# The tail unit of the first batch becomes a group of its own at the beginning of the second exponential phase

## The chip, the cores and the metric

The kernel runs on one core of a Trainium2 chip. The metric is the device time of one execution in microseconds (us), lower being better. Five engines work side by side, each through its own instructions in a fixed order: TensorE (PE) for matrix products and transposes, VectorE (DVE), ScalarE (ACT), GpSimd (POOL) and SyncE (SP). POOL and SP issue the transfers. An engine waits at an instruction until the semaphores that it needs are up, and everything behind that instruction on the same engine waits with it.

## The reference

Attention with a window and a distance bias is followed by an expert layer without routing, on the attention's output.

```
batch, heads, seq, head_dim = 8, 8, 576, 64
scores = q @ k.T / 8 - slope[h] * |i - j|, kept where 0 <= i - j < 128
attn   = softmax(scores) ;  x = (attn @ v), heads joined: 4608 tokens x 512
h = x @ w_in            # 512 -> 2048
g = h * cos(h)
out = g @ w_out         # 2048 -> 512
```

Inputs and result are float32; the kernel works in 16-bit types with 32-bit sums.

## The kernel before

**Units of attention.** Each batch has 576 queries. Its work is cut into nine units: for each of four pairs of heads (`pr`) two units of 256 queries (`G` 0 and 1), and one unit `"t"`, the tail, which has the last 64 queries (512 to 575) of all eight heads. For a unit the steps are: scores on PE (L539, the tail's L529), an exponential on ACT out of the sums in PSUM (L598, the tail's L590), a multiplication by the mask with the distance bias on DVE (L623, the tail's L611), the product with v on PE (L653 and L656, the tail's L640 and L642), a division by the row sums on DVE (L694 and L696, the tail's L681 and L684), and the transposition of x into `xT`, in which x is the input of the expert layer. That last step has two forms: four or two PE transposes and a copy (`x_pe`: L742, or L729 for the tail, and the copy L752 on ACT or L753 on DVE), or a transposing transfer on SP (`x_dma`: L768, L762 for the tail). Which of them a unit takes is decided in `attention` by whether its tokens belong to a chunk (`first`) more than one chunk ahead of the phase.

**Chunks and phases.** The expert layer works through the 4608 tokens in nine chunks of 512. ACT must load a table to go from the exponential to the cosine and back, so the exponentials are gathered in phases. The program has a first phase (number -1 in the code) before any expert work, and then for each chunk c: the first half of the expert layer with its cosines (`moe1_half` L975 for chunk 0, `moe1` L782, `moe1_fast` L876), the attention phase c with `QUOTA[c]` units, and the second half (L1161 for chunk 0, L1067 later). So the "second exponential phase" is phase 0, between the cosines of chunk 0 and those of chunk 1. q and k of batches 0 and 1 are transposed by PE (`qk_transposes` L483, and copies L500 on ACT or L501 on DVE), those of later batches by SP (L396, L399) from `qnat` and `knat`, which POOL fills (L385).

**What sets the order.** The code writes the operations one after the other, but none is issued in that order. `TABLE` is a packed list of numbers: it gives the order in which `Plan.follow` takes the operations, and for those that may run on ACT or DVE it says on which. Semaphores for all dependences are then put in. So a change of one constant comes with a whole new table, and the order of all five engines is new; where a copy runs (L500/L501, L752/L753, L1052/L1053) is a choice of the table as well.

**Groups.** `attention` takes the units in twos. In a phase from 0 on, both units' scores are one operation, and the product with v of both is one operation too, unless one is a tail. In phase -1 each unit's scores are their own operation. The first phase has nine units before the change: the eight of the pairs and the tail of batch 0. The tails use two PSUM banks for the product with v.

Of the kernel before, what the change touches and what calls it, by code (L numbers as in the profile page):

```python
# [14 lines left out]
B, H, S, D = 8, 8, 576, 64  # L15
# [12 lines left out]


TABLE = (  # L30
    'c-nPV2Y6If7JmPfH!Wo*A%PHdEHqifjs=k}tV#(GFqBXPBn4$bu`FK_%_4*%1ObV(K#D*JSt&-E!h-'
    '0xDvPKfD@{Z`QYO7kX6D^JciMYzU|;fHUhcd1+;jf_Kj&N_3_w#jJy552L+3%Pc;zlP#H-yktj(-'
    'pEjqM{ck}PJwCrB3q-'
    '{9M;&d$5qHR9WADS}~;_2H1xbO#`q+wdtgon`B>6%HyG|f?3%VnDsdnr<5N0St5ZZ)?8zmXNGD<Zg2=y6N`U+Gy?'
    '$F$*GyJWJoN!r+3anTS_iMU&FrmJy)q1{k##U*rYHRJHq^Dy35b!Y@oPU}o$A?_9;n<O%5Xs0l2&{m^^1BgNm_9P'
    '~pqObs4C1TN&{Qy{6(86~%nA#%H5NW^O=4`d2vLnc~h(_}2&mQcz_^`@$G{b79x#rnLjt-93Hcj0-'
    'yv%|m2e+*e0cZK}!+72b)WUaJT8@pXD+fk0N6bOV1gB(Si4?NA5T2-'
    '!JB(zEKr!Mj%{>;HUNYjab!Z7$qCql;L3G!CjefR+FFk(bw73vr<2ntCbb8MB)_5dQYyf6J%<J=0tY;ul(MgN&rc'
    'O0s&EiG$uIcm#Y~Vab;v#yqnaVrE7GY>V-A}Btqa`;P_Nv&jvF#{*7WM`>VMkre&#)Wy?uO_aV#gax-'
    'm{4=v5trFP6j>R?Tw2c0rY#J*M(j<PaOY>o)>#w^hUa2)xJ2kX>J~-'  # L40
    '#3SczLYEI#)13`0UMgZCvSU&r@KXVhQx8AYHOt^~S#t385v1pL)39f1&X4(!RY_VSn%~;N7Le~0Vt5k)3C!7qncH'
    'Sb_KKyP6<WQBL=(H{om`}^2hwehkBNkN1f6-'
    '=6Jf`#n1*9F&|{#~8ip5b`?XFO3>mnmKg4fqM&X#D2BXTu`vb#MxEL-'
    '2=FZh<=U!>)?uhVjo~ev?pC0h90j^d!W2#$W>Vg}3Lez;yMB~`dF58D5!*GHZ4bkokcrZJo8XMBIs3+J`c0!*&!='
    'cNak2M(+9t6%k<c;_TI5&xT-;_~SjMe)zLQ?kr-'
    '9G)}so_oZgT~!nS)>B%(>F{i(nL<%Kma6dPT_kIY8xqVGm@6sSZY)QY;}3kyZHF!JjrNbPWohF6A1kpQae^Jz>4Y'
    'nMq|4ag_#Z%abX$X0Qx{bdg5-'
    'w!C^Sy0wzSSv6YO*7!5g5KOZPW>L)jeqDWi^PVfHiNt_&bV&I7<#pb?el1f*R3lvbBscPqQM6(|M=#E!7MQtWiEo'
    '^$q8jetWg{{laSk`ID;w6<lHL!It@CI3ZRWxET-dy=6bdfZi^BN)-'
    'kx6rkxYh^Af7Y$CX%W0qP@nf!;+_cuy#JAV$$(>L5)aS8M@n1a32RRL3Yb{W0a`!VJ8|o4{JEnxs(L});p(&v8a9'  # L50
    'u_yO{KZHL$YuW?tu(Sy-'
    '!vCGTmAdZpg4wXLtycpkG<<E5@OtDZg=!_1h1+Njmjw*z0aL)7QnhFOPv(elHPlI>oe%EXgvk}suL+RHI+l!oPEe'
# [43 lines left out]
class Plan:  # L96
# [63 lines left out]
    def follow(self, text):  # L160


        raw = zlib.decompress(base64.b85decode(text))
        n, at, self.order = len(raw) // 2, 0, []
        assert n == len(self.all)
        for lo, hi in zip(raw[:n], raw[n:]):
            at = (at + lo + 256 * hi) % 65536
            o = self.all[at % 32768]
            if isinstance(o.fn, dict):
                e = "dve" if at >= 32768 else "act"  # L170
                o.fn, o.eng = o.fn[e], (e,)
            self.order.append(o)

# [79 lines left out]
def bass_alibi_sliding__then__act_gcu_kernel(  # L253
# [8 lines left out]
    with ExitStack() as ctx:  # L262
        def sb(name, shape, dt=BF16):
            return ctx.enter_context(nc.sbuf_tensor(name, shape, dt))

        R = Plan(nc, ctx)
# [20 lines left out]
        xT = sb("xT", [128, NPAIR, XR], F16)  # L287
# [7 lines left out]
        qB = {w_: gsum[:, 2304 * i:2304 * i + 2304].bitcast(BF16).rearrange("p (y c) -> p y c", y=2)  # L295
              for i, w_ in enumerate("qk")}
# [1028 lines left out]
```

## Time and profile before

| | before |
|---|---|
| median of three runs | 300.12 us (299.69 to 300.17) |
| profiled execution | 299.71 us |
| its span | 298.0 us |
| PE busy | 287.9 us, 97% |
| DVE busy | 262.1 us, 88% |
| ACT busy | 222.1 us, 75% |
| POOL busy | 95.2 us, 32% |
| moved by the DMA engines | 37.96 MB |
| TensorE clock granted | 1.00 |

The span is the time from the first to the last instruction of the profiled execution; 1.7 us lie around it in that execution's time. A busy row is the sum over the instructions of an engine. In a row of the timeline stand the start, the length, the engine, the line, the operation, and behind `x` how many like instructions follow one another; in brackets stands how long the engine had waited before, and whose result ended that wait. Matrix products overlap in PE's pipeline: the length of a row holds the last one's passage, so the pitch of a stream is read from starts.

### The profile page before, as it was taken

The numbers are of one execution on the slowest core, as the hardware profiler recorded it, in microseconds if no ns is written. First come the engines' busy times: TensorE is split into PE (matmuls) and PEld (weight loads), VectorE is DVE, ScalarE is ACT, GpSimd is POOL, SyncE is SP. The second block draws the span as 40 slices with busy tenths as digits, with TensorE's granted clock in tenths as the row PEclk, the third lists the DMA queues.
The fourth block names the chain that finished last, engine by engine and source line by source line (L and its number), as shares of the span: only waits on it lengthen the run. The fifth ranks groups of instructions, "written<-read, shape, count | busy, mean of one in ns | idle before, by whom it ended". The sixth has DMA issues, their size and how long they took to land.

```text
span 298.0 us, 7278 instructions
## 1 busy us (share of the span) xinstructions
PE 287.9 (97%) x2974; PEld 205.2 (69%) x2974; DVE 262.1 (88%) x522; ACT 222.1 (75%) x318; POOL 95.2 (32%) x122
## 2 busy tenths in 40 slices
PE   2899999999999999999999999999999999999996
PEld 2678845446874586458854788547768888888884
DVE  3879877599977999899999999999999999999972
ACT  5788878689757889688777878579778758778620
POOL 7997000599642303991195005000000000000000
PEclk9999999999999999999999999999999999999999
DMA  7999999999999994999999939973131400041033
GB/s 153 173 205 208 207 169 146 180 196 155 136 175 147 130 187 90 142 173 173 169 170 133 163 85 130 159 164 74 21 79 21 150 2 0 2 141 37 10 134 106
DMA packets 147729, 37.96 MB, mean 127 GB/s; under 512 B 133360, under 2 KB 146416, under 8 KB 147696
## 3 DMA queue, kind: packets, MB, share of 16 engines
q0 software_dynamic: 99344, 18.10, 79.7%
q1 hardware_dynamic: 48352, 19.41, 34.5%
q8 instruction: 23, 0.38, 0.5%
q14 instruction: 10, 0.08, 0.1%
HBM read 36.70 MB, written 9.44 MB: 155 GB/s over the span
## 4 chain that ended last, share of the span: by engine, by line
PE 94%; DVE 2%; POOL 1%; issue 1%; ACT 1%; POOLq 0%; DVEq 0%
PE ps L1067 33%; PE ps L782 24%; PE ps L876 11%; PE ps L539 5%; PE ps L975 5%; PE ps L1161 4%; PE ps L653 3%; PE ps L656 2%; PE ps L742 2%; PE ps L483 2%; PE ps L529 1%; DVE kt L501 1%; PE ps L640 1%; PE ps L642 1%; PE ps L1138 1%
## 5 line engine op out<-in xcount | busy, mean ns | idle before, releaser
L1067 PE MATMUL ps<-w_outb,gT 128*128 128x256 f16 x512 | 82.3, 273 | 0.0
L782 PE MATMUL ps<-xT,w_inb 128*128 128x512 f16 x336 | 82.2, 379 | 0.0
L787 ACT ACTIVATE cos<-ps,halfpi 128x512 f32<-128x512 f32 x84 | 54.9, 687 | 18.9 <-PE ps L782 13.9
L598 ACT ACTIVATE p<-ps 128x768 bf16<-128x768 f32 (+1 forms) x64 | 55.6, 915 | 11.5 <-PE ps L539 9.5
L791 DVE TENSOR_TENSOR gT<-ps,cos 128x512 f16<-128x512 f32 x84 | 54.5, 686 | 5.5 <-ACT cos L787 5.1
L1067 PEld LDWEIGHTS ps<-w_outb,gT 128*128 128x128 f16 x512 | 48.2, 98 | 12.5 <-issue 1.3
L782 PEld LDWEIGHTS ps<-xT,w_inb 128*128 128x128 f16 x336 | 31.7, 98 | 31.1 <-DVE gT L791 1.5
L375 POOL DMA_DIRECT2D vp<-in_v_dram x40 | 34.3, 892 | 53.1 <-PE ps L656 35.3
L1067 PE MATMUL ps<-wsum,gsum 128*128 128x256 f16 x256 | 38.5, 273 | 0.0
L623 DVE TENSOR_TENSOR p<-p,emask 128x768 bf16<-128x768 bf16 (+1 forms) x64 | 38.0, 615 | 0.3
L385 POOL DMA_DIRECT2D qnat<-in_q_dram x30 | 25.5, 918 | 23.9 <-DMA qt<-qnat 23.9
L1052 ACT ACTIVATE ob<-ps 128x512 f32<-128x512 f32 x33 | 19.6, 598 | 13.7 <-PE ps L1067 11.2
L385 POOL DMA_DIRECT2D knat<-in_k_dram x30 | 25.7, 948 | 9.3 <-DMA kt<-knat 7.0
L1067 PEld LDWEIGHTS ps<-wsum,gsum 128*128 128x128 f16 x256 | 23.2, 98 | 4.0 <-issue 0.5
L876 PE MATMUL ps<-xT,w_inb 128*128 128x256 f16 x132 | 24.8, 273 | 0.0
L696 DVE TENSOR_TENSOR xnats<-ps,rec 128x256 f16<-128x256 f32 x56 | 21.9, 420 | 0.5
L539 PE MATMUL ps<-qt,kt 64*128 64x128 bf16 (+1 forms) x320 | 20.1, 253 | 1.3 <-DVE kt L501 1.3
L653 PEld LDWEIGHTS ps<-vp,p 128*128 128x128 bf16 x256 | 16.0, 99 | 4.3 <-issue 1.0
L653 PE MATMUL ps<-vp,p 128*128 128x65 bf16 x256 | 18.9, 196 | 0.1
L1067 PE MATMUL ps<-wsum,gT 128*128 128x256 f16 x112 | 18.1, 273 | 0.0
L539 PEld LDWEIGHTS ps<-qt,kt 64*128 64x128 bf16 x320 | 11.9, 98 | 8.6 <-issue 3.6
L1161 PE MATMUL ps<-w_outb,gT 128*128 128x512 f16 x64 | 17.6, 380 | 0.0
(111 smaller groups left out, 478.0 us busy)
## 6 DMA issues: line engine op xcount, KB each, us to landing
out_dram<-ob SPq DMA_DIRECT2D x35, 256.0 KB, 2.7
vp<-in_v_dram POOLq DMA_DIRECT2D x32, 128.0 KB, 6.9
qnat<-in_q_dram POOLq DMA_DIRECT2D x24, 128.0 KB, 7.1
knat<-in_k_dram POOLq DMA_DIRECT2D x24, 128.0 KB, 10.8
w_inb<-in_moe_w_in_dram POOLq DMA_DIRECT2D x4, 512.0 KB, 10.5
w_outb<-in_moe_w_out_dram POOLq DMA_DIRECT2D x4, 512.0 KB, 21.8
gsum<-in_q_dram POOLq DMA_DIRECT2D x1, 576.0 KB, 15.5
gsum<-in_k_dram POOLq DMA_DIRECT2D x1, 576.0 KB, 17.6
```

What stands on the lines that cost most here:

```text
L375: op("pool", [lambda e, t=t, rows=rows: e.dma_start(vp[b % 2][0:rows, t, :, 0:64], v[b, :, 128 * t:128 * t + rows, :].rearrange("h p d -> ...
L385: fns.append(lambda e, t=t, rows=rows: e.dma_start(nat[which][b % 2][0:rows, t, :, :], src[b, :, 128 * t:128 * t + rows, :].rearrange("h p ...
L539: ins = e.matmul(ps[:, banks[x], c0:c1], keys_ap(b, x, pr, kc), query_ap(b, x, pr, qb, 128 * nb), start=c0 == 0 and (b, pr, G) not in seed ...
L598: op("act", lambda e: e.activation(P[i][:, :, 0:hi], src_[:, :, 0:hi], ACTF.Exp, scale=0.125), w=held + [("P", i)], occ=920 if G else 691, ...
L623: op("dve", lambda e: e.tensor_tensor(p, p, m, ALU.mult), r=[("EM", h0), ("EM", h1)] + ([] if G else [("EM2", h1)]), w=[("P", i)], occ=600 ...
L653: ins = e.matmul(o, P[i][:, x, d0:d0 + 128], V[:, kc, h, 0:65], start=True, stop=not two)
L782: op("pe", lambda e, kc=kc: e.matmul(ps[:, bank, :], w_in[:, kc, 128 * fc:128 * fc + 128], xT[:, kc, r0:r0 + CH], start=(kc == 0), stop=(k ...
L787: op("act", lambda e: e.activation(cosb[ci][:, :], ps[:, bank, :], ACTF.Sin, bias=halfpi[:, 0:1]), r=["halfpi"], w=[("B", bank), ("cos", c ...
L791: op("dve", lambda e: e.tensor_tensor(gT[gi][:, fc, :], ps[:, bank, :], cosb[ci][:, :], ALU.mult), r=[("cos", ci)], w=[("B", bank), ("g", ...
L876: op("pe", lambda e, i=i, kc=kc: e.matmul(ps[:, bank, 256 * i:256 * i + 256], left(kc, p0 + i), right(kc), start=(start and i == 0 and kc ...
L1067: op("pe", lambda e, t=t, p=p: e.matmul(ps[:, bank, 256 * t:256 * t + 256], left(p, slice(128 * t, 128 * t + 128)), right(p), start=(start ...
L1161: op("pe", lambda e, t=t, fc=fc, bank=bank: e.matmul(ps[:, bank, :], gT[gi][:, fc, 128 * t:128 * t + 128], w_out[:, fc, :], start=(fc == 0 ...
```

## The change

The constant `QUOTA[0]` goes from 8 to 9 units and the first phase takes eight units instead of nine. A table `TRI` gives the sizes of the first groups of a phase: phase 0 begins with a group of one, which is the tail of batch 0, and goes on in twos. Since the tail's phase is now 0 and its tokens lie in chunk 1, `first > phase + 1` no longer holds for it, and its x goes by `x_pe` instead of `x_dma`. `TABLE` is new as a whole; the other edits make the group sizes a list.

```diff
 TABLE = (
...
-                e = "dve" if at >= 32768 else "act"
+                e = "dve" if at >= 32768 else o.eng[0]
...
-        QUOTA = [8, 10, 10, 12, 14, 9]
+        QUOTA = [9, 10, 10, 12, 14, 9]
...
+        TRI = {0: [1]}
...
         def attention(us, phase):
 
-            for g in range(0, len(us), 2):
-                two = us[g:g + 2]
+            sizes = TRI.get(phase, [])
+            sizes = sizes + [2] * ((len(us) - sum(sizes) + 1) // 2)
+            for i, size in enumerate(sizes):
+                g = sum(sizes[:i])
+                two = us[g:g + size]
...
-                    if g // 2 < SEEDN.get(phase, 0):
+                    if i < SEEDN.get(phase, 0):
...
-        attention(every[0:9], -1)
-        done = 9
+        attention(every[0:8], -1)
+        done = 8
```

In the changed file the lines stand 7 to 11 further down: L590 is L598 there, L598 is L606, L975 is L983.

PE at the end of the first phase, from the second pair's product with v (L656) to the first expert products; before:

```order
L656 MATMUL ps<-vp,p 128x65
L539 MATMUL ps<-qt,kt 128x256 x2
L539 MATMUL ps<-qt,kt 128x128 x4
L742 MATMUL ps<-ident,xnats 128x128 x8
L539 MATMUL ps<-qt,kt 128x256 x2
L539 MATMUL ps<-qt,kt 128x128 x4
L529 MATMUL ps<-qt,kt 128x64 x16
L975 MATMUL ps<-xT,w_inb 128x256 x7
```

and now:

```order
L664 MATMUL ps<-vp,p 128x65
L750 MATMUL ps<-ident,xnats 128x128 x4
L547 MATMUL ps<-qt,kt 128x256 x2
L547 MATMUL ps<-qt,kt 128x128 x4
L983 MATMUL ps<-xT,w_inb 128x256
L750 MATMUL ps<-ident,xnats 128x128 x4
L547 MATMUL ps<-qt,kt 128x256 x2
L547 MATMUL ps<-qt,kt 128x128 x4
L983 MATMUL ps<-xT,w_inb 128x256 x12
```

The tail's 16 products (L529) are gone from here, and one expert product moved ahead of the last transposes and scores.

ACT in the same place, from the second pair of exponentials to the table of the cosine; before:

```order
L500 ACTIVATE qt<-ps 128x4x32x5
L598 ACTIVATE p<-ps 128x2x384 x2
L598 ACTIVATE p<-ps 128x1024 x3
L752 ACTIVATE xT<-ps 128x256 x3
L590 ACTIVATE ptail<-ps 128x1024
L598 ACTIVATE p<-ps 128x1024
L752 ACTIVATE xT<-ps 128x256
L980 ACT_TABLE_LOAD
```

and now:

```order
L508 ACTIVATE qt<-ps 128x4x32x5
L606 ACTIVATE p<-ps 128x2x384
L508 ACTIVATE kt<-ps 128x4x32x5
L606 ACTIVATE p<-ps 128x2x384
L606 ACTIVATE p<-ps 128x1024 x2
L760 ACTIVATE xT<-ps 128x256
L606 ACTIVATE p<-ps 128x1024
L760 ACTIVATE xT<-ps 128x256
L606 ACTIVATE p<-ps 128x1024
L988 ACT_TABLE_LOAD
```

The tail's exponential (L590) left; a copy of transposed keys (L500, formerly one of DVE's L501) came to ACT, and two of the copies to `xT` went elsewhere.

PE where phase 0 begins, between the last products of chunk 0's first half (L975) and the first scores of batch 1; before:

```order
L483 MATMUL ps<-ident,gsum 64x128 x16
L975 MATMUL ps<-xT,w_inb 128x256 x7
L1161 MATMUL ps<-w_outb,gT 128x512 x2
L640 MATMUL ps<-vp,ptail 128x65
L642 MATMUL ps<-vp,ptail 128x65
```

and now:

```order
L491 MATMUL ps<-ident,gsum 64x128 x16
L983 MATMUL ps<-xT,w_inb 128x256 x11
L1169 MATMUL ps<-w_outb,gT 128x512 x5
L491 MATMUL ps<-ident,gsum 64x128 x16
L537 MATMUL ps<-qt,kt 128x64 x16
L1169 MATMUL ps<-w_outb,gT 128x512 x12
L547 MATMUL ps<-qt,kt 128x256 x2
L547 MATMUL ps<-qt,kt 128x128 x2
```

Before, the tail's product with v (L640, L642) stood here; now its scores (L529) do, and its product with v and the transposes of its x (L729, four of them) come behind the first scores of batch 1.

More of the change, by code (lines that the diff above doesn't have):

```diff
@@ L38 @@
[L38 to L52, printed above, removed]
@@ new lines @@
+    'PRx1#wipsW2&0QZI+rrmw_yEnwGF8!`QcsjSc-+E7o9{#=ezxpHoHajOBH-'
+    'G=TwwoSucrE{|`QGbqJa#6duFnI$n9oI<>qxDW7QK>gMUPS?X_33>oH3*t{bIC6_I%7tN!1wX8$Z3Adq;+zUI`f|'
+    'Mwd(L+&hlWlYfQBKOlqJeNZqcfLho!N;j^hU(Q!_E84)vkR!Sk2ss&290%D^F<<XbRxRnJq`l|;oymOVLY;quF1%'
+    'Xjcfk)h7h2;huHrkX<7%{lwZfI<+%S9^RmInFWm;YMqh@VTwf7au`^JZt1A4FP94Li$XyKhcp9Y_6I?Ct!X$?MT8'
+    't|<Le^JBx)1GvGyCH9FA+?^LgM`ms&AUGDx*u-'
+    'Nf#O`)(D8Upb<jYYn?fVgX~(=2>ZFo`>s!aRH?0_QYI$=ID!zO`)aUkMbf>6K3g|^;VH(#9KP8m5OiWWrgbK9(-'
+    'vuQU?W0tQXVh}8O1Yv;rq{|eam53o^5k}$Y0h@*slc_5eh^>^0%{XdF!kOa5LbNld<x!(OU3ICdZfr(J(4%f`}5}'
@@ new lines @@
+    'P^uje=N*qa%ZQ4qZ+$-'
+    '9pmf!aRHqH@z*D3595wm~(LUioezHduTx*~1<qOO9EW}(v+>6_egBV7+{#D=_$#W8u1#Fq4AZ{0Fbg4mM8B1D&^i'
+    '=XbUyYK7~gv0H7GxnGNk`1KiI3ao8CeKu?DO_8Ct^1P>&zf~}E_DKkx&6+anN`83fJleGEGb<rzA@`m#I;2?J}eo'
+    'bn0;w!<KjlA2k}jhF8Dor9iqrQC{;2IUq4Q(ney)`goxbxiZM_bhJ<cvT~k2+kfYQ=ry28HY2bEE@43%c@Sty+K6'
+    '%;2F0X%#QYm;V&guEP;?dwEKN+El`F-'
+    '+meMC3({0QEg>!ck8gk#A^L0@+<{X0|#k=D2e&cfn2&rE+&N$k6K$%_IfYSHKlZE$_?u~jF<ey8Jmqy?eU<Ev_;f'
+    'PCSQtZOZ=N}C}6B(5k?wm;)g1d28TdAbA~+q`|x0n#5XuGVVS$q%hN5LF>qB}Z-=a5VXVA-'
@@ new lines @@
+    '(;g+8|hUF&z)5R=ju0Y4fzj4h@ShoZIbrJ@|#7&KqZgo2N8&9skPxXmrs(bI<#qcl1^i{{<(G+{L``&}pfsRH-'
+    '4;r8j06xN=_OvOQ75ytkSsW6|erLDwI6bzp#Bce0_zPfD`>!7ZIuRvZYWu1DE&A*Ds&emD;8<J?-'
+    '6DuEQERA?Q$B}))gGzgiX9XxRl5BrcI-'
+    '68<~Me1G%gcL&rq^Ju)|7+6<Y19&q;h*osI4x0D_7!(N>!=AdOwgii8L1GL*0H3&M6~d<+d@)vuAP<PKt)8oFD|V'
+    'n97G;BTz+;ywMk#wmWn&KQVy<{6m(=lb7-A(SNw?GJ9cKFv{yT#cj^q6?5+EhF?-'
+    '{IV_Ui^D0kJQ$EhbnI?u%&8sFx$7y(PJE*xJv=o1p*za%!aRopP|`h2Pu0Wk*dFG;gJs)K4*QX#(DmEyClJF}E3N'
+    'c%qeoIB%N*{FwlFYkjRg07L!f4qq`hZ5Q)1ERV>wOnl&g(I<Qw+^B!t^$|Xjmqar91c4l&2vZWp76_U%0ZP9*@^B'
@@ new lines @@
+    '$-HyVo2R8200@5~-'
+    'TMLf%Ww`a^<VRxjk$w`r06HNKt;4px_{Gzayco#XpRr#+1E+N|!Kap|9Qo>ma3xoPu8N2<VQ_h*Oj8mIIOiwjZ9w'
+    'rrN=fYVF+fM9e?uVJuB7HgRD}Vj5;b)yesZC6*uivK{0KIERMw*r2j;x%l%(9~l;8Qk-zSzwig)+ACW-'
+    'O+zmo}^SsMVg{P46tp6GNCq?W`Ac4g|2mqFH;w`TWV;J%kOH?1Hozte%*k)I^ky@TumK<2(rHvQpNwzw*_Xwd(%_'
+    'qFa22kp5P+ouKAe3zTGb0glpn|r};`xLR?8NsH_-'
+    'Po{xtWw1_aK-&)(T~PI`*G=GpHsonSyQwv!WW~zUeNJ<RI}{Hhv*(Ppp|(|KO(#Qfk-VFoO8cN#z#=Dmt)(Y+Fjn'
+    'P6e@8jiT9gKM*x)YcxsJE(!1dA#XwMXV$mvn?J8k8X_9!t>!Rd&1!HJ1pBN#<#bqFh2&g6i=NAH3J{ALguU@-'
@@ new lines @@
+    '27(jQCoSqQ`l8tOOP(C;iaau%piM$9Xx^Z@8{P7ZjC_sXqN`as~u2Q<3-'
+    'n}%kW7#{QQ3j)6?TOI*Bw+KOKao5Iwu`rX6RNALJJ^5_K_uP}Nt~@Ox*I(^EV?ZIy}zL}N3MQYn(Nl>q#*(<(?mC'
+    '3eQWg7S2M>GpI`qt*Z1cKz|fD~^LTfrzCT1HAlD~z7q(`5{z`SZdVcEV0*~iIl!M0;OnPdVR2<cU3BzSe-'
+    'tKsc3BO(TuG-c*R`J6`+4`(um%SYa*CX`A_I#pcaU)Z(?ffgO-Gyz1SW63yq|$H4_Igsmd$*B{)<pNFSMQ8Wf1Pk'
+    '_-'
+    '5%%8#C3;=P1a;xWcmCr5P|Z@{@Sn!zfIT`{`2GtM2ZVujokXh?ZoN?6nRVgDly|*Wb7vq1T^XlT!gq3B_0kz&xFI'
+    'FxQ$<Y>0SHp3vv=rxu)-wehrQT^BdO|jKoXtd&?bb0=MmW+%(ZAAH%#gIPJU?N5?NiH5SvuPD|!CjC-'
@@ new lines @@
+    'YTUyF`*e#{_&_P6}+nH?UshC?=*A?%8<bNTWUhKm1Rh8=36e8IBl)W1GT}_DGK>HhN-Zvou~@!Vy!e-'
+    '_`U_lo>J&X^^5M=NkGV#}f{RLy<3K{H1^BHplXql}T~3GA++WEApYTvP=(DW)@}bGmqhzjX0!_7}6e1ZaL;AMcJm'
+    'ZPDm~ThaO@X&vIsaV=^_n;LsyXH)CFkX-'
+    '!#Yq92W+m|QS==(o&?D3c9ke$QN~aWe8XM`1Ik7y+5wP|Ts`r5h~PW(T&R7Hn;fIGLH2rBFt6C`+Jb>@A6+Y%o%c'
+    'kQq?e+ExfD131iOnrCKVXk9-'
+    'eG>Vx`mTQ|KBfS>?6gXzCFumAknZpc=V}+K(2#%QzD_d+`jC3<VFyY1ulC^j?NhmA8HU`;N!34&R@f0g;vp<dvL2'
+    'HPx6$42FMgLOvWM|TbRRZQWWQe)n0BhJx5HmCFprsq8>5LD?CY!1ho4@ue;V}6{*;CyHt<4#SttxCf*#NQ>wY4r;'
@@ new lines @@
+    'pt0Ca)0W~e>BCs5`D;}t2LCwLxNS<tW-'
+    '&W5io>Kl#ZEoNWF5t}F)ok|qsbfw<`Z)QTl^GDxtJn}VU9&|Snx1CQ5+_wcAi<Zv}q#)AzKL&hEl8q7zxTCz0DQ%'
+    'U*&-%K{ndh=>!W_W;exL8M|p+s-<LXS!2=>Y)>Y_TUlr9Hu?jrq8SYape&l&-'
+    'wZ)vRy{>A(?PMeE?ZuVTO@0funDtOgRJYfQvxQJ>?U9u*lmc+q%!l)U@}V$?DA;brCD;upn;|07y+2THpv{rxw(q'
+    'jGq8>bc6!7T2a7nf3Ct>Rc8)mgnm5m40-'
+    'wXiij*mX)T|BN6g*>@j7@>Vlt9*2Ocy>_;z!>gu3#1&S{UeQVcsW=ErWTK(Z={}36f%MZmdWtI~ibYW2}vxK}I%s'
+    '6vzG`!mJ2WhvmFQnGZxvl3Gtj?36M*+fkCk`G0J(t1?R!GA${)!lXF%hZSb#8Cx-H9OM7L_~iTtYrgIy'
```

49 lines of the change are left out of this document (11 added, 38 removed).

## The prediction

> **What bounds the kernel now.** I read the page first: the busy rows, the slices, and the chain that ended last.
>
> ```profile
> PE 287.9 (97%) x2974; PEld 205.2 (69%) x2974; DVE 262.1 (88%) x522; ACT 222.1 (75%) x318; POOL 95.2 (32%) x122
> PE   2899999999999999999999999999999999999996
> DVE  3879877599977999899999999999999999999972
> DMA  7999999999999994999999939973131400041033
> PE 94%; DVE 2%; POOL 1%; issue 1%; ACT 1%; POOLq 0%; DVEq 0%
> ```
>
> TensorE (PE) is busy 97% of the span, it makes 94% of the chain that ended last, and the second row shows it full in all slices but the first two and the last. VectorE (DVE) is the next, nearly full over the last two thirds. The clock is full throughout. A stretch in which PE is already continuous can therefore only be shortened by giving PE less to do, and lengthened by giving it more; a wait elsewhere counts only where it reaches PE. Where PE is not continuous is told by the table of busy time by stretch, and by PE's own waits, which are 7.0 us in all.
>
> ```profile
> 20.00:36.00 16.00, 16.00 (x198) 13.58 (x196) 13.91 (x28) 13.23 (x22) 8.97 (x11) 1.00 1.23 207
> 36.00:52.00 16.00, 15.96 (x172) 8.58 (x170) 12.46 (x31) 12.43 (x19) 0.00 (x0) 1.00 2.08 162
> 260.00:280.00 20.00, 20.00 (x185) 17.73 (x184) 19.10 (x26) 15.67 (x21) 0.00 (x0) 1.00 0.20 66
> PE ps L483 <- POOL ident L421: 5.7, 1, 5.7
> PE ps L539 <- DVE kt L501: 1.3, 2, 0.9
> ```
>
> The columns behind the stretch are the busy times of PE, its weight loads, DVE, ScalarE (ACT) and GpSimd. From 20 us on PE has no gap worth naming. The change acts inside the first 52 us, so the sum has two parts: what PE is spared or gains before about 18 us, where it still waits, and what it gets to do more from 36 us on, where every nanosecond of PE counts. The two timelines of the start show the first part (columns: start, length, engine, line).
>
> ```profile
> 13.50 1.04 PE L539 MATMUL ps<-qt,kt 64*128 64x256 bf16 x12 [0.38 <-DVE kt L501]
> 16.99 0.61 PE L539 MATMUL ps<-qt,kt 64*128 64x256 bf16 x6
> 17.39 0.64 PE L529 MATMUL ps<-qt,kt 64*128 64x64 bf16 x16
> 17.96 0.94 PE L975 MATMUL ps<-xT,w_inb 128*128 128x256 f16 x7
> 10.57 0.88 ACT L500 ACTIVATE qt<-ps 128x640 bf16<-128x640 bf16 x1
> 12.07 1.51 ACT L598 ACTIVATE p<-ps 128x768 bf16<-128x768 f32 x2 [0.62 <-PE ps L539]
> 14.21 2.85 ACT L598 ACTIVATE p<-ps 128x1024 bf16<-128x1024 f32 x3 [0.63 <-PE ps L539]
> 18.07 1.02 ACT L590 ACTIVATE ptail<-ps 128x1024 bf16<-128x1024 f32 x1 [0.17 <-PE ps L529]
> 21.26 1.28 ACT L980 ACT_TABLE_LOAD   x1
> ```
>
> The tail's scores (L529) are the last thing before the first expert product (L975) at 17.96, from which PE runs on without a stop. The tail's exponential is one of nine on ACT before it turns to the cosine.
>
> **What the change removes at the start.** PE gets rid of the 16 products of L529. They begin at 17.39 and the row behind begins at 17.96: 0.57 us, of which one change of tile form (from 64*128 to 128*128) stays, since L539 now stands there. That change of form is priced from a later place, where everything is hidden:
>
> ```profile
> 102.23 0.27 PE L1067 MATMUL ps<-w_outb,gT 128*128 128x256 f16 x1
> 102.43 0.50 PE L539 MATMUL ps<-qt,kt 64*128 64x256 bf16 x8
> 102.87 1.16 PE L1067 MATMUL ps<-w_outb,gT 128*128 128x256 f16 x9
> 114.49 0.41 PE L529 MATMUL ps<-qt,kt 64*128 64x64 bf16 x16
> 114.73 0.33 PE L539 MATMUL ps<-qt,kt 64*128 64x256 bf16 x4
> ```
>
> A stream of L1067 starts one in (1.16 - 0.27) / 8 = 0.11 us, but L539 starts 0.20 behind the one at 102.23: 0.09 goes into the change of form. Its eight products take 0.44 us to the next L1067; four of 256 columns and four of 128, with two halves of the array side by side, make 0.32 at the same rate, so the way out costs 0.12. Hence 0.57 - 0.12 = 0.45 us leaves PE at the start. The order of the new kernel also puts one L975 ahead of the last transposes and scores, done while those wait: 0.11. Together 0.56 us earlier, if the path to 17.96 is PE's or shortens as much elsewhere.
>
> Is it? ACT's row of the new order sheds the tail's 1.02 us, but takes over one L500 copy (0.88 by the row at 10.57) between the third and fourth exponential, in a place where ACT waited 0.62 and 0.63 us. Placing the same durations one behind the other, exponentials of 0.75 and 0.95 each, ACT would end its sixth at 15.75, the first xT copy at 16.1, the last exponential at 18.6 and load its table at 18.6 instead of 21.26. The first L975 could go at 16.3 and the unbroken stream at about 17.5 with one product already done, that is 17.39 instead of 17.96. Both ways agree on 0.56. Bounds: nothing gained, if the copy on ACT delays scores by what DVE's copy did; up to PE's wait of 0.38 and the first of ACT's more, 0.56 + 0.38 + 0.62 = 1.56. I take 0.56, which both readings are nearest to.
>
> **What it adds at the beginning of phase 0.** There the tail's scores stand behind the last transposes of batch 1 and ahead of 12 L1161 products.
>
> ```profile
> 35.69 0.59 PE L1161 MATMUL ps<-w_outb,gT 128*128 128x512 f16 x2
> 36.12 0.19 PE L640 MATMUL ps<-vp,ptail 128*128 128x65 bf16 x1
> 36.70 0.64 PE L483 MATMUL ps<-ident,gsum 128*64 128x128 bf16 x16
> 37.27 1.68 PE L1161 MATMUL ps<-w_outb,gT 128*128 128x512 f16 x7
> 38.88 0.50 PE L539 MATMUL ps<-qt,kt 64*128 64x256 bf16 x8
> 38.01 1.28 ACT L598 ACT_TABLE_LOAD   x1
> 39.43 1.51 ACT L598 ACTIVATE p<-ps 128x768 bf16<-128x768 f32 x2
> 39.13 0.87 DVE L684 TENSOR_TENSOR xtail<-ps,rec 64x256 f16<-64x256 f32 x2
> 41.54 1.02 DVE L623 TENSOR_TENSOR p<-p,emask 128x768 bf16<-128x768 bf16 x2
> ```
>
> The 16 products of L529: by the row at 17.39 the way out is in its 0.57; less that 0.12, 0.45; by the rows at 114.49 and 114.73, where a like row lies between other work, 0.24. PE has no gap to hide them in; I take the larger, since it is the same unit's row. One change of form more than before (the transposes L483 leave form 128*64 anyway): 0.12. The products L640 and L642 cost the same as before, only later: 0. Sum 0.57.
>
> The Trainium skill, page TensorEngine Tiling (Array Packing), section Tiling Modes, says that a change of tiling mode drains the engine; the rows above agree, with 0.09 to 0.12 us each. The page TensorE: Matmul & The Clock Gate, section Part 2, gives some 175 ns as a constant drain, and by that, as an estimate, the change of form would cost 0.06 more than I put in.
>
> Then the tail's x. It went through SP's transposing DMA (L762), which waited 38.5 us at the head of SP's queue; now it takes four PE transposes (L729) and one more copy by ACT. The trace has four such L729 for a later batch:
>
> ```profile
> 75.69 0.23 PE L729 MATMUL ps<-ident,xtail 64*128 64x64 f16 x2
> 75.73 0.28 PE L539 MATMUL ps<-qt,kt 64*128 64x256 bf16 x1
> 75.75 0.22 PE L729 MATMUL ps<-ident,xtail 64*128 64x64 f16 x2
> SPq L762 <- DVE xtail L684: 38.5, 1, 38.5
> ```
>
> They start at 75.69 and are over, with one L539 between them, within 0.12 us, and they share the form of the scores behind them: 0.11 us. The same skill's page TensorE: Matmul & The Clock Gate, section Part 4: PE-mode transpose, gives about 275 ns for one transpose in a kernel; taken as occupancy, that would be an estimate of 1.1 us for the four and a net loss of 1.2 us. The trace's starts do not bear it out.
>
> What is owed in phase 0 is 0.57 + 0.11 = 0.68 us; the start was split differently (the second-piece transposes L483 in two groups of 20 with scores between), two more pairs of form changes there, which I put at 0.1 after what ACT's waits hide. Owed 0.78, gained 0.56: **0.2 us slower**.
>
> **What else moves.** The first scores of batch 1 stood at 38.88, and follow 12 instead of 7 + 2 products of L1161 now, at about 40; ACT, which turns to the exponential at 36.2 by the same laying end to end, has loaded the table and done the tail's exponential by 36.2 + 1.28 + 1.02 = 38.5. Behind them the tail's L640 and its xtail on DVE stand ahead of the masks of batch 1; the next L653 has some 3.5 us from its scores in the new order and needs 0.5 + 1.5 (two exponentials) + 0.9 (xtail) + 0.5 (mask) = 3.4: it just fits, with 0.1 to 0.3 lost if not. SP and POOL: SP no longer holds transposes of batch 2 behind the tail. POOL loads q of batch 4 ahead of k and q of batch 3; batch 3's first scores are those at 102.43.
>
> ```profile
> 69.27 4.98 SPq L396 DMA_TRANSPOSE qt<-qnat  x1
> 80.23 5.86 SPq L396 DMA_TRANSPOSE kt<-knat  x1
> ...
> L1053 DVE COPY ob<-ps x2: 684/684/684, 115.2 to 212.9; 128x512 f32<-128x512 f32 x2
> ```
>
> Batch 3's were issued at 69.27 and 80.23, 11 us apart, so one step later the second of them is issued at about 91 and over, with the 5.9 of its first part and 2 to 3 for the second and the landing, at about 99: still ahead of 102.43, with 3 us of cover left. Finally three more copies of output sums go from ACT (L1052) to DVE (L1053, 0.684 us each), two of them close together among the last 25 rows of DVE's order, ahead of its last L943, where DVE has 0.9 us idle between 260 and 280. They cost PE nothing while DVE stays ahead of it; without that cover the two of the last chunk cost up to 2 x 0.68 = 1.37.
>
> **The rivals.** (a) Faster: PE loses its waits at the start wholly, the upper bound of 1.56 gained against 0.78 owed: 0.8 less, 299.3. For it speaks that ACT is ready with its exponentials 2.66 us earlier; against it that the weights of the products are still arriving in that stretch (the DMA row shows 9 in its slices). It decides where the unbroken L975 starts before 16.9. (b) Slower, the DVE copies: the last products wait for DVE's last gT (L943), and two copies stand in DVE's queue before it; for it speaks DVE's 19.10 of 20 us, against it that the order also takes ACT work out there. Half to all of the 1.37 reaches PE: 0.7 to 1.4, about 301.3. It decides where DVE comes to that L943 later than PE to its product. (c) Slower, supply: batch 3's transposes arrive later than its scores; each us late costs one. It decides at a landing after 102.4; 301 to 304. (d) Nothing at all within the measurement: the terms cancel to under 0.1, since all are tenths of a microsecond. (e) Slower, the transposes of the tail's x hold PE for a whole row each, 4 x 0.19 to 0.23 instead of 0.11: 0.7 to 0.8 more, 301.1; the starts at 75.69 and 75.75 speak against it. By the Trainium skill's figure cited above it would be this case.
>
> **How the numbers follow.** The profiled execution took 299.71 us (span 298.0), 0.41 below the median of 300.12; the sum of +0.2 gives 299.9 for such an execution and **300.3** for the median. A difference under 0.2% (0.6 us) can't be told from none here. Chances: the forecast with (d), that is within 0.6 us, 0.43; (a) 0.22; (b) 0.17, (c) 0.08, (e) 0.02, and 0.08 for the phase-0 chain and sums of small losses over 0.6: slower 0.35 in all. The range 299.2 to 301.8 reaches to (a)'s and over (b)'s middle; outside are 0.06 of (a), and (c) with the far end of (b).
>
> **What would show it.** Right: the first unbroken L975 at 17.3 to 17.5; ACT's first cosine load at 18.5 to 19; L529 as a row of its own near 37 with 0.55 us to the next row; L729 near 41; first scores of batch 1 near 40 without an idle; PE busy some 0.1 to 0.3 longer. Wrong: a wait of L653 on DVE in phase 0, a wait of scores for kt or qt near 102, an idle on PE behind 276, or an L975 row that starts where it did.

## The result and the profile after

The changed kernel takes 301.11 us (median of 8 runs, 300.61 to 301.56) against 300.13 us before (8 runs, 299.69 to 300.59): the ratio is 1.0032, with a 95% interval of 1.0020 to 1.0043. It is slower by 1.0 us. The forecast was 300.3 with a range of 299.2 to 301.8, so the time lies in the range; the likeliest case there, no change within 0.6 us, did not come, and the 0.35 for slower did.

The page of the profiled execution of the changed kernel (301.32 us, span 299.6), its busy row and PE's slices, and then, in another view, PE's own waits (line, releaser, us in total, times, longest):

```profile
PE 287.9 (96%) x2978; PEld 203.8 (68%) x2978; DVE 263.9 (88%) x527; ACT 220.2 (74%) x314; POOL 95.1 (32%) x122
PE   2789999999999999999999999999999999999996
```

```profile
PE ps L983 <- DMA w_inb<-in_moe_w_in_dram: 1.0, 1, 1.0
PE ps L547 <- DVE kt L509: 0.9, 1, 0.9
PE ps L661 <- DVE p L631: 0.2, 1, 0.2
PE ps L547 <- DVE gT L799: 0.2, 1, 0.2
```

PE's busy time is the same as before, 287.9 us, in a span 1.6 us longer. So what was lost is waits. Two of those that the view lists are new: one of 1.0 us for a piece of `w_in` in the start, and one of 0.2 us at scores (L547, behind gT) at 134 us, far behind the moved unit; the 0.2 us at L661 lies in the start, at 14.11. Smaller late starts don't show as idle time at all: a row of an L1075 product lasts 0.27 us, one starts every 0.11, and PE counts as busy as long as a row lasts. The timelines of the start (PE, then ACT's table load):

```profile
15.79 0.27 PE L983 MATMUL ps<-xT,w_inb 128*128 128x256 f16 x1
16.60 1.63 PE L983 MATMUL ps<-xT,w_inb 128*128 128x256 f16 x12
18.55 0.49 PE L983 MATMUL ps<-xT,w_inb 128*128 128x256 f16 x3
20.07 1.26 PE L983 MATMUL ps<-xT,w_inb 128*128 128x256 f16 x10 [1.03 <-DMA w_inb<-in_moe_w_in_dram]
35.74 1.24 PE L1169 MATMUL ps<-w_outb,gT 128*128 128x512 f16 x5
17.95 1.28 ACT L988 ACT_TABLE_LOAD   x1
```

The expert products begin 1.36 us earlier than before (16.60 against 17.96), and ACT loads its table 3.3 us earlier. After 16 products the first piece of `w_in` is used up and PE stands until the second has landed. The first L1161 (L1169 here) starts at 35.74; before it started at 35.69. In this execution the whole head start was spent waiting; what it is worth when the piece lands earlier, the experiments show.

PE where the tail stands now:

```profile
36.92 0.64 PE L491 MATMUL ps<-ident,gsum 128*64 128x128 bf16 x16
37.49 0.41 PE L537 MATMUL ps<-qt,kt 64*128 64x64 bf16 x16
37.83 2.76 PE L1169 MATMUL ps<-w_outb,gT 128*128 128x512 f16 x12
40.52 0.51 PE L547 MATMUL ps<-qt,kt 64*128 64x256 bf16 x8
43.28 0.23 PE L737 MATMUL ps<-ident,xtail 64*128 64x64 f16 x2
43.40 0.49 PE L547 MATMUL ps<-qt,kt 64*128 64x256 bf16 x7
```

The scores hold PE for 0.34 us (37.49 to 37.83), the transposes of the tail's x for 0.12 (43.28 to 43.40).

To see where the two kernels drift apart, I added up the streaming time of the products along each trace, the moved tail's own products left out, and compared the times at which both had done equal amounts. Against before, this trace is 0.1 us late when phase 0 begins, 0.6 to 0.7 behind it and up to 132 us, 1.1 at 143, 1.3 at 208, 1.6 at 229 and at the end. So the tail's move and its surroundings make 0.6 us here, and 1.0 us comes in steps behind 130 us, where the tail is long done. Those steps fall on single instructions at which PE starts late. The next two places are the largest of them. PE, then DVE, in the first; PE, then ACT, in the second:

```profile
133.44 0.38 PE L1075 MATMUL ps<-w_outb,gT 128*128 128x256 f16 x2
134.01 0.51 PE L547 MATMUL ps<-qt,kt 64*128 64x256 bf16 x8 [0.19 <-DVE gT L799]
132.67 1.29 DVE L799 TENSOR_TENSOR gT<-ps,cos 128x512 f16<-128x512 f32 x2 [0.28 <-ACT cos L795]
...
143.40 0.28 PE L1075 MATMUL ps<-wsum,gsum 128*128 128x256 f16 x1
143.78 0.25 PE L661 MATMUL ps<-vp,p 128*128 128x65 bf16 x3
142.65 0.60 ACT L1060 ACTIVATE ob<-ps 128x512 f32<-128x512 f32 x1
143.12 0.40 ACT L760 ACTIVATE xT<-ps 128x256 f16<-128x256 f16 x1
```

In the first, the scores write a PSUM bank which a gT of chunk 3 still reads; that gT ends at 133.96 and PE starts at 134.01. In the second, the product with v needs a bank whose transposed x ACT is copying out (L760, ended 143.52), and that copy stands behind a copy of an output sum on ACT (L1060). Both are hand-overs of a bank, 0.26 and 0.27 us longer than such a transition takes elsewhere.

### The profile page after: what moved, and what is told of

It is laid out like the page before. It is cut to its first block, busy times and chain, and to the rows that moved or that the text cites. A ratio compares the mean times of both kernels' runs of the same rounds, so it can differ in the third digit from the quotient of the medians.

```text
span 299.6 us, 7300 instructions
## 1 busy us (share of the span) xinstructions
PE 287.9 (96%) x2978; PEld 203.8 (68%) x2978; DVE 263.9 (88%) x527; ACT 220.2 (74%) x314; POOL 95.1 (32%) x122
## 4 chain that ended last, share of the span: by engine, by line
PE 92%; DMA 3%; POOL 3%; issue 1%; DVE 0%; ACT 0%; POOLq 0%
PE ps L1075 33%; PE ps L790 24%; PE ps L884 11%; PE ps L1169 5%; PE ps L547 5%; PE ps L983 4%; DMA w_inb<-in_moe_w_in_dram 3%; PE ps L661 3%; PE ps L664 2%; PE ps L750 1%; POOL vp L383 1%; PE ps L491 1%; PE ps L537 1%; PE ps L648 1%; POOL gsum L364 1%; PE ps L1146 1%
## 5 line engine op out<-in xcount | busy, mean ns | idle before, releaser
L1075 PE MATMUL ps<-w_outb,gT 128*128 128x256 f16 x512 | 82.7, 273 | 0.0
L795 ACT ACTIVATE cos<-ps,halfpi 128x512 f32<-128x512 f32 x84 | 54.9, 687 | 19.3 <-PE ps L790 14.8
L606 ACT ACTIVATE p<-ps 128x768 bf16<-128x768 f32 (+1 forms) x64 | 55.8, 915 | 12.5 <-PE ps L547 9.5
L1075 PEld LDWEIGHTS ps<-w_outb,gT 128*128 128x128 f16 x512 | 48.3, 98 | 12.1 <-issue 1.3
L1075 PE MATMUL ps<-wsum,gsum 128*128 128x256 f16 x256 | 39.7, 273 | 0.0
L1060 ACT ACTIVATE ob<-ps 128x512 f32<-128x512 f32 x30 | 17.9, 597 | 12.7 <-PE ps L1075 11.9
L1075 PEld LDWEIGHTS ps<-wsum,gsum 128*128 128x128 f16 x256 | 23.4, 98 | 4.5 <-ACT ob L1060 0.5
L884 PE MATMUL ps<-xT,w_inb 128*128 128x256 f16 x132 | 25.3, 273 | 0.0
L547 PE MATMUL ps<-qt,kt 64*128 64x128 bf16 (+1 forms) x320 | 19.5, 243 | 1.4 <-DVE kt L509 0.9
L1075 PE MATMUL ps<-wsum,gT 128*128 128x256 f16 x112 | 20.3, 273 | 0.0
L661 PE MATMUL ps<-vp,p 128*128 128x65 bf16 x256 | 18.3, 193 | 0.6 <-DVE p L631 0.2
L661 PEld LDWEIGHTS ps<-vp,p 128*128 128x128 bf16 x256 | 15.3, 97 | 5.2 <-issue 1.5
L983 PE MATMUL ps<-xT,w_inb 128*128 128x256 f16 x128 | 16.0, 273 | 1.2 <-DMA w_inb<-in_moe_w_in_dram 1.0
L1169 PE MATMUL ps<-w_outb,gT 128*128 128x512 f16 x64 | 17.2, 380 | 0.0
```

What stands on the lines that cost most here:

```text
L547: ins = e.matmul(ps[:, banks[x], c0:c1], keys_ap(b, x, pr, kc), query_ap(b, x, pr, qb, 128 * nb), start=c0 == 0 and (b, pr, G) not in seed ...
L606: op("act", lambda e: e.activation(P[i][:, :, 0:hi], src_[:, :, 0:hi], ACTF.Exp, scale=0.125), w=held + [("P", i)], occ=920 if G else 691, ...
L661: ins = e.matmul(o, P[i][:, x, d0:d0 + 128], V[:, kc, h, 0:65], start=True, stop=not two)
L795: op("act", lambda e: e.activation(cosb[ci][:, :], ps[:, bank, :], ACTF.Sin, bias=halfpi[:, 0:1]), r=["halfpi"], w=[("B", bank), ("cos", c ...
L884: op("pe", lambda e, i=i, kc=kc: e.matmul(ps[:, bank, 256 * i:256 * i + 256], left(kc, p0 + i), right(kc), start=(start and i == 0 and kc ...
L1075: op("pe", lambda e, t=t, p=p: e.matmul(ps[:, bank, 256 * t:256 * t + 256], left(p, slice(128 * t, 128 * t + 128)), right(p), start=(start ...
```

## The experiments

**Theory A**, from these lines: the loss has three parts, the weights' arrival at the start, the tail as uncovered work in phase 0, and the new order's waits from phase 1 on. **Rival B**: the move itself costs the 1.0 us, and the rest of the order is indifferent.

Since the order is a list of numbers, parts of the two lists can be joined. The code is that of the changed kernel in all of these; the joints lie at the first L1161 and at the first product of chunk 1 in PE's order.

```diff
 # e2_min
-TABLE = changed order
+TABLE = order of before to its first L1161, without the tail
+      + changed order to the first product of chunk 1
+      + order of before
 # e3_late_before
-TABLE = changed order
+TABLE = changed order to the first product of chunk 1 + order of before
 # e4_early_before
-TABLE = changed order
+TABLE = order of before to its first L1161, without the tail + changed order
```

> The changed kernel once more, for a second trace. Theory A (the loss has three parts: at the start PE now waits for the second piece of w_in, in phase 0 the tail is work that PE can't hide, and from phase 1 on the new order makes PE wait for masks on DVE): PE's wait for w_in is there again with 0.8 to 1.2 us, the waits for masks again add up to about 0.5 us, the time is 300.9 to 301.3 us. Rival B (the waits are an accident of one trace and the loss is the tail's work in phase 0 alone): the wait for w_in is under 0.4 us or the late waits lie elsewhere, at the same time.

> The changed kernel with an order put together from three pieces: up to the first L1161 the order of before without the tail, then phase 0 in the changed order up to the first product of chunk 1, then the order of before. Theory A: the start is about 0.4 us shorter than before, phase 0 0.7 to 0.9 us longer, the rest as before: 300.3 to 300.6 us. Rival B (the move itself costs the whole 1.0 us, wherever the rest stands): 301.0 to 301.2.

> The changed order up to the first product of chunk 1, and behind it the order of before. Theory A: 0.5 to 0.7 us more than before from the first 52 us and nothing later: 300.6 to 300.8 us, and no more waits for masks from phase 2 on than before has. Rival B: 301.0 to 301.2, the order of the later phases being indifferent.

> The order of before without the tail up to the first L1161, and behind it the changed order. Theory A: start and phase 0 cost 0.2 to 0.5 us together, the later phases 0.4 to 1.0: 300.7 to 301.5 us, and PE doesn't wait for w_in. Rival B: 301.0 to 301.2 with the late waits gone.

| start | phase 0 | behind | label | us | ratio to before, 95% |
|---|---|---|---|---|---|
| changed | changed | changed | e1_again | 301.04 | 1.0027 (1.0017 to 1.0037) |
| changed | changed | before | e3_late_before | 300.08 | 1.0000 (0.9988 to 1.0012) |
| before without the tail | changed | before | e2_min | 301.20 | 1.0041 (1.0029 to 1.0054) |
| before without the tail | changed | changed | e4_early_before | 301.84 | 1.0055 (1.0040 to 1.0071) |

(The kernel before stood at 299.99 us beside these; e4_early_before is four runs, the others ten.) Neither theory came out whole: e2_min came where Rival B had it, e3_late_before where neither had, and e4_early_before above both. The rows of a pair differ in one thing. Giving back the old order behind the first product of chunk 1 saves 0.96 us with the changed start (301.04 to 300.08) and 0.64 with the other (301.84 to 301.20). With the old order behind, the moved tail costs nothing that can be measured: e3_late_before is at 1.0000. So Rival B falls, and so does A's first sum, which put 0.5 to 0.7 us on the first 52 us of the changed order. What A said of e2_min was wrong by 0.7 us: with the start of before the move does cost 1.2 us. By these medians the new order of the start is worth 0.8 to 1.1 us to the changed kernel.

PE's waits in e3_late_before, where the start and phase 0 are those of the changed order:

```profile
PE ps L479 <- ACT gsum L364: 6.0, 1, 6.0
PE ps L535 <- DVE kt L497: 0.9, 1, 0.9
PE ps L535 <- ACT kt L496: 0.3, 1, 0.3
PE ps L649 <- DVE p L619: 0.2, 1, 0.2
PE ps L535 <- ACT p L594: 0.2, 1, 0.2
```

The late wait of 0.2 us is gone (the two of 0.2 that are left lie in the start, at 14.10 and 14.69), and behind 55 us this trace drifts from before by 0.1 us only, by equal work. The wait for `w_in` is gone as well, though the start's order is the changed one: it comes and goes from trace to trace. In the trace of e1_again it was 0.7 us, a little less than theory A had said, and the late waits were the same as in the first trace to within 10 ns, at all 21 places behind 53 us that I compared.

PE in e2_min, in the start and in phase 0:

```profile
17.27 0.92 PE L970 MATMUL ps<-xT,w_inb 128*128 128x256 f16 x7 [0.28 <-ACT xT L747]
18.51 0.38 PE L970 MATMUL ps<-xT,w_inb 128*128 128x256 f16 x2
19.61 1.26 PE L970 MATMUL ps<-xT,w_inb 128*128 128x256 f16 x10 [0.72 <-DMA w_inb<-in_moe_w_in_dram]
36.12 1.24 PE L1156 MATMUL ps<-w_outb,gT 128*128 128x512 f16 x5
```

With the tail's scores taken out of the old start, PE first waits for ACT's copy to `xT` and then for `w_in`; the first L1156 is not earlier than before (36.12 against 35.69). By equal work the start is 0.2 us late in this trace, in which the second piece landed 0.17 us later than in that of before, and phase 0 adds 1.05. The place that the tail left holds nothing but waits. That reading was tested by the opposite edit: the tail's scores done twice, in the kernel before and in the changed one.

```diff
 # e7_twice_start (in before), e8_twice_phase0 (in the changed kernel); in scores
                     if pr == "t":
+                        for rep in range(2 if b == 0 else 1):
                         for pr in range(NPAIR):
...
                             ins = e.matmul(ps[:, banks[x], c0:c0 + 64], ...)
```

> The kernel before with the tail's 16 score products of batch 0 done twice, where they stand, in the first phase. Theory A' (the start is bound by the arrival of w_in, so PE work ahead of it is free; this is why taking the tail away there gained nothing in e2_min): 0 to 0.15 us more than before, 300.0 to 300.2 us. Rival, the prediction's term (0.45 us leaves PE's path when they go, so it would come on when they are doubled): 0.4 to 0.5 us more, 300.4 to 300.6 us.

> The changed kernel with the same 16 products done twice, where they stand now, in phase 0. Both theories take PE as the bound there: 0.43 to 0.5 us more than the changed kernel, 301.4 to 301.6 us. If it is under 0.15 us more, phase 0 has room in it and the tail's scores cost nothing there either.

Measured: e7_twice_start 300.11 us against 300.07 for before, ratio 1.0003 (0.9991 to 1.0015); e8_twice_phase0 301.28 us, ratio 1.0043 (1.0027 to 1.0059), 0.2 us above the changed kernel, which at this spread can be told neither from none nor from the 0.43 expected. The rows (PE of e7_twice_start, then PE of e8_twice_phase0):

```profile
17.05 0.64 PE L530 MATMUL ps<-qt,kt 64*128 64x64 bf16 x32
17.62 0.94 PE L976 MATMUL ps<-xT,w_inb 128*128 128x256 f16 x7
20.10 1.16 PE L976 MATMUL ps<-xT,w_inb 128*128 128x256 f16 x9 [0.83 <-DMA w_inb<-in_moe_w_in_dram]
```

```profile
36.39 0.64 PE L491 MATMUL ps<-ident,gsum 128*64 128x128 bf16 x16
36.96 0.64 PE L538 MATMUL ps<-qt,kt 64*128 64x64 bf16 x32
37.53 1.68 PE L1170 MATMUL ps<-w_outb,gT 128*128 128x512 f16 x7
```

Thirty-two products take 0.57 us in both places, as long as the sixteen took at the start of before. There the sixteen ran at half the pace. Like products show it (before, in the start and in phase 0; then the start of e10_before_fewer_masks, a run further below with the start of before):

```profile
14.47 0.34 PE L653 MATMUL ps<-vp,p 128*128 128x65 bf16 x3
14.63 0.25 PE L656 MATMUL ps<-vp,p 128*128 128x65 bf16 x1
43.33 0.26 PE L653 MATMUL ps<-vp,p 128*128 128x65 bf16 x3
43.42 0.19 PE L656 MATMUL ps<-vp,p 128*128 128x65 bf16 x1
17.29 0.41 PE L529 MATMUL ps<-qt,kt 64*128 64x64 bf16 x16
17.65 0.92 PE L977 MATMUL ps<-xT,w_inb 128*128 128x256 f16 x7
```

Three products with v have 0.16 us to the next row at 14.47 and 0.09 at 43.33, and the sixteen scores have 0.36 in the second trace where they had 0.57. In the trace of before the half pace lasts to 17.8 us; in the other thirteen the products with v near 14.2 to 14.8 us already start one in 0.03 us. The page's granted clock (9 in every slice) doesn't show this, and no run tells what ends it. In phase 0 the second sixteen add 0.57 - 0.34 = 0.23 us. So the scores cost 0.34 us, way out included, in phase 0, and nothing that can be measured at the start.

Why nothing there, the landing of the second piece of `w_in` tells. With the start of before it is the tenth expert product that needs it: this product starts 0.04 to 0.05 us behind the landing in all five traces with that order (19.44 behind 19.40 in before, 20.10 behind 20.05 in e7_twice_start). In the changed order it is the seventeenth, 0.04 to 0.08 us behind the landing in all nine traces. What stands ahead of that product is hidden while the piece is on its way. By equal work at 35 us, with the difference in landing taken off, the nine traces with the changed start are 0.56 to 0.59 us ahead of before, and e2_min, e4_early_before and e7_twice_start are level with it within 0.01 us (e10_before_fewer_masks, whose fourth piece landed 0.86 us later, is 0.35 late). That is the worth of the new start: more work ahead of the product that has to wait.

**What makes the late waits.** Two readings were left. Theory C/D: DVE, over 93% busy from 100 us on, is behind as a whole and PE pays for its backlog. Rival E: single hand-overs stand too close in the order, whatever the amount of work. First, products were drawn ahead of the waits, in the changed order and in that of e3_late_before.

```diff
 # e5_fill_changed: 26 products, behind 53 us; e6_fill_best: at 22 waits, behind 36 us
 # PE, at one of the places (before 134.0 us)
-L1075 x2, scores L547 x8, L1075 x6
+L1075 x5, scores L547 x8, L1075 x3
```

> The changed kernel, where from phase 1 on one to three independent products of PE's own order are drawn ahead of each of the some 20 instructions that PE waited at by more than 55 ns (26 products in all); nothing else moves. Those waits add up to 2.3 us, 1.0 us more than the like ones of before. Theory A (these waits are what the change costs): 1.5 to 2.3 us less than the changed kernel, 298.8 to 299.6 us. Rival C (DVE is behind as a whole, so a wait that is filled comes back at the next instruction): at most 0.3 us less, 300.7 to 301.1 us, with the waits a little further on in the trace.

> The order of e3_late_before (the changed order up to the first product of chunk 1, the order of before behind it) with products drawn ahead of its 22 waits of over 45 ns after 36 us, 2.4 us in all. Theory A: 1.4 to 2.3 us less than e3_late_before, 297.8 to 298.7 us, faster than both kernels. Rival C: 299.8 to 300.1 us.

Measured: e5_fill_changed 300.69 us, ratio to before 1.0016 (1.0005 to 1.0027), 0.4 less than the changed kernel; e6_fill_best 300.15, ratio 1.0005 (0.9995 to 1.0014), no gain over e3_late_before. Both missed theory A's numbers by far: of 2.3 us of waits that were given something to do, 0.4 came back at most, 0.3 by equal work in the trace. In the traces the two largest places lost about 0.25 us each, but new waits stood at the next instruction, 0.2 us at the transposes of x (L742) at 114.38 and at 144.54, 0.25 at an expert product at 220.15. No version was found that beats the kernel before.

Then the work of DVE was cut (two kernels that leave out most of the mask and distance bias of eight units, so their result is another), and DVE's late copies were given to ACT.

```diff
 # e9_changed_fewer_masks (changed kernel), e10_before_fewer_masks (before); in mask
+            if b in (4, 5) and G:
+                p, m = P[i][:, :, 0:8], EM[:, h0:h1 + 1, 0:8]
-            if G:
+            elif G:
 # e11_changed_copies_act, e12_late_before_copies_act
-TABLE: L1053 and L753 behind 53 us on DVE
+TABLE: the same on ACT (L1052, L752), at the same places
```

> The changed kernel, where the eight mask multiplications of batches 4 and 5 for the units of queries 256 to 511 are cut to eight columns each (left out of the computation: the mask and distance bias of these units), 8 x some 0.55 = 4.4 us less work on DVE between about 133 and 190 us; order and all else as it is. Theory D (DVE is the bound in the late exponential phases, so PE's small waits are paid by its backlog): the waits in that stretch, 1.4 us in the changed kernel, lose 0.6 to 1.2 us: 299.9 to 300.5 us. Rival E (the order alone makes the waits, not the amount of DVE's work): at most 0.2 us less, 300.8 to 301.1 us.

> The kernel before with the same eight masks cut to eight columns (same part left out). Theory D: its waits in that stretch are 0.4 to 0.5 us, so 0.2 to 0.5 us less, 299.5 to 299.9 us, and less than the changed kernel gains. Rival E: within 0.2 us of before, 299.9 to 300.2.

> The changed order with the ten copies that DVE makes behind 53 us (four of output sums, six to xT; 4 x 0.68 + 6 x 0.28 = 4.4 us) given to ACT, at the same places of the order. Theory D: DVE is relieved, 0.2 to 0.6 us less than the changed kernel, 300.4 to 300.8 us, unless the copies wait longer on ACT. Rival (b) of the prediction (the added output copies alone make the loss): 0.7 to 1.0 less, 300.0 to 300.3. Rival E: 300.9 to 301.2.

> The order of e3_late_before with its eight late copies on DVE given to ACT (two of output sums, six to xT, 3.0 us). Theory D: 0.1 to 0.4 us less than e3_late_before, 299.7 to 300.0 us, the best so far; rival E: 300.0 to 300.2 us.

| label | us | ratio to before, 95% |
|---|---|---|
| e9_changed_fewer_masks | 301.52 | 1.0054 (1.0041 to 1.0067) |
| e10_before_fewer_masks | 300.00 | 0.9994 (0.9974 to 1.0015) |
| e11_changed_copies_act | 301.88 | 1.0065 (1.0052 to 1.0078) |
| e12_late_before_copies_act | 305.55 | 1.0193 (1.0179 to 1.0207) |

(The kernel before: 299.91.) Only e10_before_fewer_masks came where a theory had put it (rival E); the other three lie above every range, e12 by 5 us. DVE is busy 3.5 and 3.8 us less in the traces of e9 and e10, and neither kernel gained: by equal work e9 loses 0.98 us behind 130 us, as the changed kernel does, and e10 gains 0.01 on before. So theory D falls. Giving the copies of e11 to ACT made things worse, but moves work to ACT as well, so it doesn't clear the added output copies of the prediction's rival (b) by itself. The steps do: nearly all of the 1.0 us lies between 130 and 230 us, where DVE copies one output sum in either kernel (at 213 us before, at 214 now; the others stand at 115 before, and at 53, 248, 275 and 277 now). Behind the last two there is a late start of 0.18 us, at 281.91, which is gone in e11. The rest of the time of e9 isn't explained; in its trace the second piece of `w_in` landed last of all, at 20.29. Why less work on DVE gained nothing, the trace of e9_changed_fewer_masks shows at the place around 143 us (PE, then ACT):

```profile
143.68 0.28 PE L1077 MATMUL ps<-wsum,gsum 128*128 128x256 f16 x1
144.06 0.25 PE L663 MATMUL ps<-vp,p 128*128 128x65 bf16 x3
142.93 0.60 ACT L1062 ACTIVATE ob<-ps 128x512 f32<-128x512 f32 x1
143.41 0.40 ACT L762 ACTIVATE xT<-ps 128x256 f16<-128x256 f16 x1
```

The wait is still 0.27 us (0.273 with the whole masks, 0.271 now), and so are the others behind 130 us, to within some 20 ns, because PE never waited for the masks here but for the copy of x on ACT, behind an output copy. I followed thirteen of the changed order's late waits back to the work on which they depend and which ended last. Two end at the unit's own mask; the other eleven end where another engine has done with a PSUM bank: four at a division, two at ACT's copy of x, two at a gT, two at sums that DVE adds out of PSUM, one at an exponential. That work ended 0.06 to 0.26 us before PE started. That it counts where a copy stands in ACT's order, e12_late_before_copies_act shows in the large (PE's waits):

```profile
PE ps L535 <- ACT p L594: 2.0, 3, 1.3
PE ps L1063 <- ACT ob L1048: 1.8, 2, 1.3
PE ps L649 <- ACT xT L748: 1.0, 1, 1.0
```

Eight copies, 3 us of work, moved to an engine with room, at places that were chosen for another engine, cost 5.5 us, more than the work itself. What stays open is the single waits' own share of the 0.96 us: no run moves one of them alone, and e5_fill_changed shows that filling one shifts a part of it to the next.

## Why the prediction was right or wrong

- **What bounds the kernel, and that PE is full from 20 us on.** Right behind 20 us: PE has the same work but for four transposes, and what was lost is late starts. "The clock is full throughout" is the page's granted clock; by the pace of its products PE ran at half speed up to 17.8 us in that trace, and it is from there that the start's prices were read.
- **The 0.45 us that leave PE at the start.** Wrong twice. The 0.57 us from 17.39 on is the price of the half pace; e10 has 0.36 for the same products, and e7_twice_start fits twice as many into 0.57. And PE's time there is not on the path: what comes behind is fed by `w_in`, and the tenth expert product starts when its second piece has landed. The term is 0 with the old order of the start, not 0.45 (e2_min).
- **The 0.56 us in all, checked by laying ACT's work end to end.** ACT did better than laid out, with the table load at 17.95 against my 18.6, and the first unbroken L975 came at 16.60 against 17.3 to 17.5. That is earlier than the 16.9 that the prediction made the sign of rival (a), and still the time went the other way. For I did not ask what the products would wait for next: I had named the arriving weights only as an argument against rival (a). By equal work up to phase 0 the changed start was 0.1 us late in the first trace and 0.6 early in that of e3_late_before, as the second piece landed later or earlier. At equal landing it is 0.56 to 0.59 early, so the 0.56 was hit almost to the digit, by luck: it is not time that PE is spared, but work that the new order has ahead of the product that waits.
- **The price in phase 0, 0.68 us.** The pieces were 0.34 for the scores, way out included, where I had 0.57 (the larger of two rows, which was the one at half pace; the 0.24 of the row at 114.49 was the right one, and e8_twice_phase0 gives 0.23), and 0.12 for the transposes, where I had 0.11. The Trainium skill's rule of the drain (page TensorEngine Tiling (Array Packing), section Tiling Modes) is borne out by 0.34 - 0.23 = 0.11 us for the way out. The 275 ns per transpose of the Trainium skill's page TensorE: Matmul & The Clock Gate, section Part 4: PE-mode transpose, are not what one costs here: four passed within 0.12 us. So rival (e) falls. By equal work phase 0 costs 0.56 to 0.80 us in the traces with the changed start, where 0.78 was owed. Beside 0.46 for these pieces there is a late start of 0.20 us at the first product with v (PE, then ACT):

```profile
43.83 0.39 PE L1169 MATMUL ps<-w_outb,gT 128*128 128x512 f16 x1
44.24 0.25 PE L661 MATMUL ps<-vp,p 128*128 128x65 bf16 x3
43.60 0.38 ACT L760 ACTIVATE xT<-ps 128x256 f16<-128x256 f16 x1
```

It starts 0.41 us behind the row before it, where products like that one start one in 0.22, and 0.26 behind the end of ACT's copy, as at 143.78. Of this place the prediction had said "it just fits, with 0.1 to 0.3 lost if not", and the sum had it at 0.

- **Start and phase 0 together, 0.2 us slower.** e3_late_before has exactly these parts changed: +0.1 us, interval -0.4 to +0.4. Right within what can be told: gain and price have about the sizes of the sum, the gain for another cause.
- **"What else moves": nothing for the new order from phase 1 on.** This is the step that failed, the 0.96 us (0.98 to 1.00 by equal work behind 130 us, in four traces with this order). I checked the supply of batch 3, the output copies and one place in phase 0, and put zero on the rest of an order in which all five engines were new. Rivals (b), the DVE copies at the end, and (c), the transposes of batch 3, didn't come: of (b) there are the 0.18 us at 281.91, where PE waits for a sum of DVE's behind the copies and not for its gT, and nowhere does PE wait for a transpose of batch 3. The 0.08 that I gave to "the phase-0 chain and sums of small losses" was the case that came, and it was too little. That the time lies in the range is owed to bounds drawn for (a) and (b); the sum itself missed by 0.8 us.

## What to carry to other kernels

Where a change comes with a whole new order, its own terms and the new order are two changes, and the second has a spread of its own: here 0.6 to 1.0 us out of 300, more than any term of the edit. It should get a line in the sum and a chance, and joining the two orders at a boundary tells the two apart in one run. Work placed ahead of a load that had not arrived was free here: before crediting its removal, double it, or ask what its successor will wait for next. And before a row gives a price, compare its pace with a like row elsewhere in the trace: the row at 17.39 ran at half of it.

## What the runs showed of the hardware

The second piece of `w_in` was issued within 0.3 us in all fourteen traces (9.6 to 9.9 us), but landed between 19.3 and 20.3 us, and the start follows it: nine traces with one and the same start order reach the first L1161 between 34.98 and 36.01. How long PE ran at half pace differed as well, with one order too: products with v near 12.4 us started one in 0.03 us in the first trace and one in 0.05 in that of e1_again. By equal work the first trace and that of e1_again, one order, are 0.08 to 0.10 us apart from 23 us to the end, and their late waits repeat to 10 ns. So a trace's own time carries the luck of its start, and differences between two traces are to be read behind it.
